# Local attention output in one matmul form for all four batches, under a newly searched instruction order

## The chip, the cores and the metric

The kernel runs on one core of one Trainium2 chip. The metric is device time in microseconds (us) from the first to the last instruction of a run, as the device reports it; the numbers below are medians of runs of the whole kernel. One run of each kernel was also recorded by the hardware profiler, and every row in this document comes from that recording.

## The reference

```python
def _attn_ref(q, k, v):                      # (4, 8, 576, 64)
    factor = 4; Sd = S // factor; scale = 1.0 / np.sqrt(D)
    q_d = q.reshape(B, H, Sd, factor, D).mean(axis=3)      # k_d, v_d alike
    out_d = sm_attn(q_d, k_d, v_d)           # full attention over 144 means
    out_up = np.repeat(out_d, factor, axis=2)
    mask = np.abs(pos[:, None] - pos[None, :]) < factor
    scores = np.where(mask, scale * q @ k.T, -1e9)         # a band of 7 keys
    out_local = softmax(scores) @ v
    return out_up + out_local
x = attention, as 2304 tokens x 512
h = x @ w_in;  g = h * clip(h + 3, 0, 6) / 6;  x = g @ w_out         # d_ff 2048
return max(x @ w1, x @ w2, x @ w3) @ w_out2                          # d_ff 768
```

## The kernel before, in words

**Stages.** There are four batches, b = 0 to 3, and two halves of 288 tokens each. Attention of batch b has a pooled part (`down_scores`, `down_pT`, `down_out`) and a band part (`local_scores`, softmax on DVE and ACT, `local_out`). The two wide layers of the first network follow: for batches 0 and 1 in quarters g = 0 to 3 of the 2048 columns (`moe1_h`, matmuls at L1273, and `moe1_y`, L1311), for batches 2 and 3 by a Strassen-like scheme (L1436 and L1527). The second network, three token groups long, ends the kernel (L1848 and L1957). Large products are made of float16 high and low parts; the attention's are float32.

**The band output.** `local_out(half, e)` multiplies the softmax weights of 12 blocks by 32 keys of v each. One call of it covers two pairs of heads (`cc` = 0, 1, so c = 2e + cc) and the two heads of a pair (`hl` = 0, 1), 48 matmuls of 32 rows by 64 columns in all. A matmul's rows of the array are chosen by c (`tile_position` row 32c) and its columns by hl (column 64 hl). Its result goes to the PSUM tile `pts[cc]`, its moving operand is `pl{half}{hl}`. So in a listing the number of the tile `at` tells the row group and the number of `pl` the column group. In a float32 matmul the trace has two records for one instruction: 96 records are one call. The four batches issue the 48 matmuls in four different orders, chosen by `[b]` at the end of a list of orders; `local_scores` does the same for its matmuls (L964).

**Order.** Every operation is recorded with its number; the text `ORDER` lists the numbers in the order in which they are issued, a star picks the other engine of two that may do an operation (mostly GpSimd in place of VectorE), and `.1` puts in one idle matmul on `warm` (L2091). Each engine then works through its own instructions strictly in that order and waits by semaphores. The costs given to `op(...)` are not read by `schedule`, which only follows `ORDER`.

**The start.** SP issues all DMAs, in order. `load_vw` (L815 to L830) brings v for the band output; for batch 0, half 0 it first clears 32 rows on GpSimd (L815), and SP's own L823 waits for that. Weights arrive as 64-bit numbers: raw tiles `y2` and `y3`, loaded at L1158, are turned to float32 by ACT (L1130), GpSimd (L1132) and DVE (L1135), squared and summed on ACT (L1175) for a scale, and split into high and low float16 parts (ACT L1232, DVE L1234). The softmax of the band ends on DVE with L981 and L984, then L1021 (DVE or GpSimd) and a transpose, L1023. `L1062` adds the band output to the pooled output, and `split` makes x16 of it.

Of the kernel before, what the change touches and what calls it, by code (L numbers as in the profile page):

```python
# [185 lines left out]
0-1 5 7 2 18 22 6 72 23 67 222 38 139 4 213 19-20 9 3 10-11 8 12 15-16 21 13 24 14 17 26 28 25* 35 37 74 36 27  # L186
29 31-33 30 69 86 88 87 89 34 93 68* 92 70* 43 91 44-47 71 98 90 75-76 99 77 94 78 100-101 39 79-80 95 81-82 40
104 103 105 102 48-49 55-56 50 57 51 83 231 73* 96* 214 41 106 216 58 224 215 59 52 97 110 113 60 107 109* 223
53 111 226 54 61 227 62-63 160 115 162 64 161 163 114 112* 108* 116 218 119 118 165 84 167 117 166 85 164 120
65* 66 140 219 172 42 220 217 228 168-169 174 845 225 173 121* 221 175 229 122-123 230 247-248 141 239 178 170  # L190
249 124 250-254 171 235-236 184 176 233 237 177 185 232 179 125-126 234 255-256 127 238 180-181 142-143 187
144-145 391 257 392 128-129 244 183* 241 130 132 131 240 243 245 182 269 186 242 273 135 150-151 146 189 271 275
246 403 276 258-259 393 188 844 397 136* 270 272 147 394 190 148 191 152 260 133 193 192 261 134 277 287 262 395
295 137 194 138* 399 263 195-197 846 288 398 153 264-265 149 266-267 274 154 402 268 859 289-290 282 278 285 198
296-298 400 291 847 155-157 292 158* 303 159 280 283 199 860 405 540 304 293 305 299 281 279 300 311-312 306 313
848 404 201 408 200 314 881 294 849 286 406 301 401 302* 307 284 308 409 315 850 202 862 319-320 316 861 309 317
310* 318* 856 539 851 203 852 209 858 210 857 853 863 321-322 410 323 .1 339 204-206 855 411 407 396 412 207
347-348 208 211 324-325 854 413-414 541 326 329 415-421 212* 542 422-423 543 327 340-342 328 349 343-344 545
334-336 868 424 870 428 865 350 330-332 355 426 351 425 337 864 356-358 345 429 352 867 346* 353 359 338 333 363
427 364 869 926 365-367 360-361 866 433 547 371 871 551 434-436 376 354 927-929 368 873 877 906 550 430 362 546  # L200
548 874 369 441-442 377 372 931 437 875 872 907 438 932 930 933 370* 443 908 431 934 432 935 552 439 449 878 444
373 882 912 883 374 450-451 884-887 375 879 445-446 909 452 556 453 457-458 381-383 459 447 911 914 544 378-380
553 936* 937* 440* 888 876 894 554 889 895 454 915 896 880 558 950 460-461 938 448* 897* 487-488 384 386 939-940
890 489 387 557 385 455 462 941 898 463 891 942 945 944 951 495-496 559 465 953 955 456 892 943 490-491 497-499
388 560 466-467 899 893 464* 900 492 1000 389-390 946 1002 500 901 1001 549 947 952 503-506 954 555 471 511-512
468 1003 1006 493 910* 904* 902 948* 561 916 903 917 1476 472 979 562-564 905 473 513 474 694 565-568 913* 949*
494* 469 569-571 1005 1004 1007 514 980-981 507 475 508 572-573 1008 576 477 956 959-960 515 478 958* 482
982-983 1009 1011* 984-985 990 986 991 483 580-581 484 582 479 688 1477 1487 501 578 509 957 502* 1010* 987 510*
1012 485 480 1475 961* 992 574 516-517 988 1480 588 1478 1481 918 579 583 1479 1482 577 1491 589 1484 689 691
518 481 575 1483 1488 584-585 486 519-522 590 1485-1486 586 919 591 524 690 525 1013 993 526 596 1489 592  # L210
920-921 597 1495 1492 1014 593 1493 695 594 1502 1494 1496 604-606 989 994 598 523 607 922-925 1015 595 1531 692
699 587 1499 529 696 599 1500 1497 600 1490 601 1498 602 962-964 527 697 700 1501 702 608 634 1018 530 1503-1504
635 531 636 965-967 609 968 642-643 1017 1019 1016 610 701 698 528 969 1024 644 532 1027 637 611 533 995 998 703
1020 1551-1552 1021 534-537 1553-1554 1028 538 1029* 1026* 1025 638 970-971 704 972 996* 603* 973 639 1023*
1022* 470 997 1555 1558 1557 1556 1559 612-613 1560 974 645 614 617 640 650 615 646 1534 1030 1033 1032* 1034
999 616 1035 618 1507-1509 1031 1532 1562 1537 1561* 1036 619-620 623 705 693 1539 706-707 1037 647 641 621 708
476 622 1533* 1038 648 1510 709 1511-1513 1575 651 1519 624 652 625-626 1577 1514 710-712 653 1520 1536 1576 713
629-630 714 1521 715 654 627 716-717 1515 718-720 1540 655 1522* 1516* 649* 1563 666 631 1578 1565 1580 1579 721
1517 1564 1566 658-661 1044-1046 722 656 1523 1569 723 1568 662 1518 1047-1048 1524 632 667 731-733 1505 663
1039 1041 1040 739 664 1570 724 1535 734 657 1525 665 668 1567 735 1042 633 725 669 740-742 670 1571 1526 743  # L220
1572 736-737 672 1541 1043 1542 1527 673 1543 747 674 1621 744 1622 1538* 1573* 1544 675 755 748 1623 1545 1053
756 677 1624 1529 1528 1628 1627 1625 749 678 1581 1583* 1626 679 750 757-758 751 1546 759 1530 1601 745
1602-1604 738* 1574* 1629 1547 628 1548 671 746* 728 726 729 752 676 1549 1630 1632* 1672 760 682 1584 680 786
1673 1582 1586* 1585 753 683 794-795 684-685 796 1605 727 1506 681 1631* 1550 754 1606 1587-1588 1611 761 686
975 1589 977 763 787 1612-1614 762* 788-792 730 1607-1608 1590 769-770 764 797 1592 1591 1633 798-800 1635 1634
1636 1593 771-773 1594 1640 801* 1671 978* 765 802 766 1637 1639 1638 793* 810 803 811 1645 812 1647 1683 767
804 1641-1642 976 1685 1644* 775 805 813 1684 1646 806 1677 776 1049 1678 780 777 1674 807-808 1679 1675 687 814
1609 778 1054-1055 1654 1676 815 1680 1610 1056-1057 1656 809 781-783 1062 1686 1690-1691 1058 1655 1059 779
1070 1687 1071 1682 816 1681 1688 1063 1689 1072 1600 1595 817* 1643* 1596-1597 784 818-819 1064 1615-1617 1598
1651 1051 1599 820 1653 1704 1652 1618 1648 821 1695 1650 1619* 1620 1697 1649 822 1060 1692 1065 1696 1073 824  # L230
1657 1066 1658 1061* 1694 1067 1050 823 1052* 768 1659 1693 1068 1078 831 1749 1751 1074 1698 1075 1750 1701 825
1106 826 774 1752 1700 827 1079 832-834 1080 1703 1702 1699 828 1754 1756 1755 1660 1662 1661 1081 1753
1757-1759 837 1107 1663 835 1076 1069* 1077* 1664 1761 1108 1705 838 1109 1086-1088 1773 1082 1708 1729-1730
1083 1735 1084 1706 1763 1760 1762 1707 1764-1765 1768 1766-1767 1114-1117 1776-1777 1774 1110 1778 1775 839
1769 1819-1820 1111 1821 1770 1822 1734 1665 1667 1825 1824 1823 1826 1122 840 1123-1125 1666 1709 1085
1118-1119 1827 1669 1772* 829 1771* 1710 1828 1112 1113* 1829* 1731* 841 1737 1732 1120 1126 1130 1091 1738 1668
1131 1089-1090 1830* 1121* 1127-1128 1129* 836 1711-1714 1779 1092-1093 1715 1782 1094 1096 1781* 1132-1133 1158
1095 1719 1733* 1780 1720 1716 1831 1784 1134 1833 1670 1832 1135 1159 1097 1101-1102 1098 1160-1161 1783 1162
1739 1834 1740-1741 1136 1137* 1736* 1163 1099 1166-1167 1742 1174-1175 1100 1835 1721 1717 1838 1168 1103 1176
1104-1105 1837 1138 1169-1170 1836 1164 1743-1745 1722 785 1746-1748 1785-1786 1718 1723-1724 1727* 1171 1725  # L240
1177 1787 1839 1798 1182-1183 1143-1144 1843 1846 1178 1165* 1840 1868 1179 1139 1844 1140 1184 1841* 1847 1842
1845 1848* 1849 1726 1210 1728 1852 1185 1141 1799 1186 1850 1172 1800-1802 1173 1211-1213 1851* 1142 1187 1854
1853 1180 1855 1803 1856 1804 1809 1218 1145-1146 1148 1805-1806 1181 1214 1857 1807 1147 1808 1810-1811 1188
1788 1790 1789 1149 1791 1153-1155 1792-1793 1795 1812-1813 1215 1814-1815 1794 1796 1226-1228 1219-1221 1216
1816 1817* 1189* 1797 1818 1858 1860 1222 1859 1223 842 1217* 1224-1225 1156 1861-1862 1229 843 1150-1151 1863
# [169 lines left out]
def kernel(  # L415
# [73 lines left out]
    T = {}  # L489
# [1642 lines left out]
```

## Time and profile before

| | |
|---|---|
| median of 3 runs | 789.91 us (789.42 to 791.1) |
| profiled execution | 790.44 us |
| its span on the core | 788.7 us |
| TensorE matmul (PE) busy | 740.1 us, 94% |
| VectorE (DVE) busy | 557.5 us, 71% |
| ScalarE (ACT) busy | 471.1 us, 60% |
| GpSimd (POOL) busy | 304.9 us, 39% |
| mean granted clock of TensorE | 0.97 |

A busy share is a mean over stages with different limits, so each stage has to be read by itself. The profiled execution's own time lies 1.7 us above its span: what stands around the first and the last instruction.

### The profile page before, as it was taken

To read this page: it belongs to the slowest core of one execution; us is meant where nothing else is said; L and a number is where in the kernel's file an instruction comes from. 1 tells how busy PE (TensorE), PEld (TensorE's weight loads), DVE (VectorE), ACT (ScalarE), POOL (GpSimd) and SP (SyncE) were. 2 spreads that over 40 slices of the span, in tenths; PEclk is the share of its full clock that TensorE was granted. 3 is DMA by queue.
4 is the path that set the end of the run, shared out by engine and by line. 5 is a ranking of instruction groups with operands and counts; after the bars stand their busy time and mean duration, and the time that the engine had idled before them with its cause. 6 is when DMAs were issued, how large, how long until landed. Compare 5 with 4: busy or idle time off the path is not lost.

```text
span 788.7 us, 20630 instructions
## 1 busy us (share of the span) xinstructions
PE 740.1 (94%) x8491; PEld 554.3 (70%) x8491; DVE 557.5 (71%) x1139; ACT 471.1 (60%) x1065; POOL 304.9 (39%) x338
## 2 busy tenths in 40 slices
PE   4668899998999999999999999999999999999998
PEld 3455676876777787777777777775555766677667
DVE  1749888788674668888864487368999547852783
ACT  4648899775647535448975588449826441543153
POOL 4525366765433523456342115234654302510050
PEclk9656999999999999999999999999999999999999
DMA  9278856624082000003556333305100010000102
GB/s 259 76 221 229 215 170 168 175 76 82 3 157 74 16 4 2 2 1 101 149 163 197 119 104 110 105 1 173 68 1 2 28 41 14 1 27 1 41 1 94
DMA packets 81248, 68.43 MB, mean 87 GB/s; under 512 B 56962, under 2 KB 68226, under 8 KB 81154
## 3 DMA queue, kind: packets, MB, share of 16 engines
q1 hardware_dynamic: 81154, 67.12, 30.4%
q8 instruction: 66, 1.08, 0.6%
q14 instruction: 28, 0.23, 0.1%
HBM read 56.10 MB, written 11.01 MB: 85 GB/s over the span
## 4 chain that ended last, share of the span: by engine, by line
PE 76%; DVE 12%; ACT 6%; issue 2%; DMA 2%; POOL 1%; SPq 0%; ACTq 0%; DVEq 0%
PE y L1527 12%; PE y L1311 9%; PE h L1273 9%; PE a L1848 8%; PE y L1848 8%; PE at L1957 7%; PE a L1436 6%; PE y L1436 3%; PE h L1848 3%; PE at L1042 2%; PE at L759 2%; PE h L1436 1%; PE a L964 1%; ACT junk L1175 1%; PE at L921 1%
## 5 line engine op out<-in xcount | busy, mean ns | idle before, releaser
L1273 PE MATMUL h<-x,wi 128*128 128x288 f16 x768 | 118.9, 291 | 0.6 <-DVE gf L1288 0.6
L1311 PE MATMUL y<-g,wo 128*128 128x288 f16 x768 | 115.7, 286 | 1.4 <-DVE x L1062 0.7
L1848 PEld LDWEIGHTS <-m2ow 128*128 128x128 f16 x756 | 73.9, 98 | 52.9 <-issue 5.1
L1527 PE MATMUL y<-ga,wo 128*128 128x288 f16 x768 | 96.3, 286 | 0.0
L1527 PEld LDWEIGHTS <-wo 128*128 128x128 f16 x768 | 75.1, 98 | 19.0
L1273 PEld LDWEIGHTS <-wi 128*128 128x128 f16 x768 | 73.7, 99 | 21.0 <-issue 1.8
L1311 PEld LDWEIGHTS <-wo 128*128 128x128 f16 x768 | 72.8, 98 | 21.0 <-issue 3.1
L1848 PEld LDWEIGHTS <-m2w 128*128 128x128 f16 x378 | 36.8, 98 | 22.3 <-DVE hm L1862 0.2
L1293 POOL TENSOR_TENSOR g<-gf,g 128x288 f16<-128x288 f32 x34 | 29.6, 872 | 50.4 <-ACT g L1291 37.3
L1132 POOL TENSOR_SCALAR z<-z 128x384 int32<-128x384 uint32 (+1 forms) x36 | 22.8, 632 | 62.3 <-DMA z<-in_moe_w_dram 37.9
L1848 PE MATMUL y<-yb,m2ow 128*128 128x384 f16 x234 | 43.6, 326 | 2.2 <-DVE hm L1862 1.7
L1848 PE MATMUL a<-yb,m2ow 128*128 128x384 f16 x234 | 43.4, 326 | 1.4 <-DVE hm L1862 0.7
L1436 PEld LDWEIGHTS <-S 128*128 128x128 f16 x384 | 37.4, 98 | 9.6 <-issue 0.2
L1135 DVE SCALAR_TENSOR_TENSOR zo<-zo,z 128x384 int32<-128x384 int32 (+1 forms) x36 | 21.1, 587 | 21.0 <-ACT zo L1130 16.0
L1957 PE MATMUL at<-m2fw,hm 128*128 128x256 f16 x288 | 35.0, 272 | 0.6 <-DVE y L1976 0.6
L1957 PEld LDWEIGHTS <-hm 128*128 128x128 f16 x324 | 31.7, 98 | 5.5 <-issue 1.0
L1291 ACT CAST g<-gf 128x288 f16<-128x288 f32 x64 | 27.3, 430 | 12.8 <-DVE gf L1288 10.0
L1436 PEld LDWEIGHTS <-wi 128*128 128x128 f16 x288 | 28.2, 98 | 7.1
L1346 POOL TENSOR_TENSOR m2fw<-hm 128x384 f32<-128x384 f32 x7 | 7.9, 1140 | 57.1 <-DVE hm L1862 48.7
L1284 ACT ACTIVATE r<-h,sc 128x288 f32<-128x288 f32 x32 | 18.8, 592 | 18.4 <-PE h L1273 18.4
L871 ACT ACTIVATE pd<-a,dsm 72x144 f32<-72x144 f32 x60 | 22.1, 376 | 11.5 <-DVE dsm L865 9.2
L759 PE MATMUL at<-ident,stg 128*128 128x128 f32 x128 | 22.2, 314 | 7.1 <-DVE stg L656 2.3
(331 smaller groups left out, 1824.5 us busy)
## 6 DMA issues: line engine op xcount, KB each, us to landing
z<-in_moe_w_dram SPq DMA_DIRECT2D x24, 384.0 KB, 3.3
y<-in_moe_w_in_dram SPq DMA_DIRECT2D x8, 1024.0 KB, 5.8
y<-in_moe_w_out_dram SPq DMA_DIRECT2D x8, 1024.0 KB, 5.3
vw<-in_v_dram SPq DMA_DIRECT2D x62, 96.0 KB, 4.1
out_dram<-y SPq DMA_DIRECT2D x18, 256.0 KB, 2.2
stg<-in_k_dram SPq DMA_DIRECT2D x6, 512.0 KB, 6.0
stg<-in_q_dram SPq DMA_DIRECT2D x6, 512.0 KB, 7.1
stg<-in_v_dram SPq DMA_DIRECT2D x6, 512.0 KB, 4.6
```

The lines of the kernel that those rows point to most:

```text
L759: nc.tensor.transpose(out=po[:, i, :, f], in_=T[n(f"{nm}{kc}{c // 2}")][:, f, 2 * (c % 2):2 * (c % 2) + 2, :], identity=ident[0:nr, 0:nr])
L871: op("ACT", c_act(SD, 2) - 0.01, prio, lambda i=i, j=j, x=x: nc.scalar.activation(out=T[pds[j]][:, i], in_=view(j)[:, i], func=AF.Exp, bia ...
L1132: op("POOL", c_f32(n), prio, lambda: nc.gpsimd.tensor_scalar(out=words()[0], in0=words()[0].bitcast(U32), scalar1=0.8735 * 2.0 ** -29, sca ...
L1135: op("DVE", c_dve(n), prio, lambda: nc.vector.scalar_tensor_tensor(out=dst().bitcast(I32), in0=dst().bitcast(I32), scalar=3, in1=words()[0 ...
L1273: nc.tensor.matmul(out=hp(), lhsT=T[wt][:, a, kk, i * P:i * P + P], rhs=T[x16][:, e, kk, :], start=(kk == 0 and (a, e) == (0, 0)), stop=(k ...
L1291: op("ACT", c_act(CH, 0, False), prio + LEAD, lambda: nc.scalar.copy(out=T[g16][:, 0], in_=T[gf]), r=[gf], w=[(g16, 0)], new=[buf(g16, "ac ...
L1293: op("DVE", c_dve(CH), prio + LEAD, lambda e: e.tensor_tensor(out=T[g16][:, 1], in0=T[gf], in1=T[g16][:, 0], op=ALU.subtract), r=[gf, (g16 ...
L1311: nc.tensor.matmul(out=T[acc][:, 0:CH], lhsT=T[wt][:, a, i, d * P:d * P + P], rhs=T[gs[i]][:, e], start=(i == 0 and (a, e) == (0, 0)), sto ...
L1436: nc.tensor.matmul(out=ps_(x)(), lhsT=lhs(a, kt), rhs=T[xn][:, e, kt, :], start=(first and kt == 0 and (a, e) == (0, 0)), stop=(kt == 1 an ...
L1527: nc.tensor.matmul(out=T[acc][:, 0:CH], lhsT=T[wt][:, a, 2 * fb + i, d * P:d * P + P], rhs=hl[:, e * S + half * CH:e * S + half * CH + CH] ...
L1848: nc.tensor.matmul(out=b(to), lhsT=w_op(nm, o)[:, a, kt, fp * P:fp * P + P], rhs=T[f"yb{p}{y}"][:, e, kt, :], start=(first and kt == 0 and ...
L1957: nc.tensor.matmul(out=ps_(x)(), lhsT=h_op(p, fp, o)[:, a, i * P:i * P + P], rhs=T["m2wo"][:, j, e, fp, :], start=(first and fp == 0 and ( ...
```

## The change: one form, and another order

Three things are edited. `local_out` now issues its 48 matmuls in the one order that batch 1 had; `local_scores` in the one that batch 0 had. Two costs given to the planner are lowered, which `schedule` doesn't read. `ORDER` is replaced as a whole (141 lines); of its numbers one line stands here before and after, since numbers tell a reader little. The new one has two entries `.1` where the old one had one.

```diff
-0-1 5 7 2 18 22 6 72 23 67 222 38 139 4 213 19-20 9 3 10-11 8 12 15-16 21 13 24 14 17 26 28 25* 35 37 74 36 27
...
+3874 3854 3878 3855-3858 3884-3887 3879 3888 3880-3883
...
             for kc in range(2):
-                op("PE", 0.7, prio, lambda kc=kc: pe(kc), duty=0.36, ni=32,
+                op("PE", 0.6, prio, lambda kc=kc: pe(kc), duty=0.36, ni=32,
...
                     for o, nq in spans_:
-                        for hl, c in (
-                                [(hl, c) for hl in range(2) for c in range(4)],
-                                [(hl, c) for c in range(4) for hl in range(2)],
-                                [(c % 2 ^ x, c) for x in range(2) for c in range(4)],
-                                [(hl, c) for c in (0, 2, 1, 3) for hl in range(2)])[b]:
-                            nc.tensor.matmul(
...
+                        for hl in range(2):
+                            for c in range(4):
+                                nc.tensor.matmul(
...
             def pe(j):
                 ii, two = range(4 * j, 4 * j + 4), range(2)
-                for i, hl, cc in (
-                        [(i, hl, cc) for i in ii for cc in two for hl in two],
-                        [(i, cc ^ x, cc) for i in ii for x in two for cc in two],
-                        [(i, hl, cc) for hl in two for i in ii for cc in two],
-                        [(i, hl, cc) for cc in two for i in ii for hl in two])[b]:
+                for i, hl, cc in [(i, cc ^ x, cc) for i in ii for x in two for cc in two]:
...
             for j in range(3):
-                op("PE", 0.6, prio, lambda j=j: pe(j), duty=0.11, ni=64,
+                op("PE", 0.48, prio, lambda j=j: pe(j), duty=0.11, ni=64,
```

In the changed kernel lines after the 955th stand 3 to 6 lower: L964 is L961, L1042 is L1036, L1135 is L1129, L981 is L979, L984 is L982, L1158 is L1152. Lines between 189 and 955 stand 1 higher.

**TensorE, the band output.** Batch 2, half 1, before: the column group (`pl`) stays while the row group (`at`) alternates.

```order
L1042 MATMUL at_3885<-pl_3741,vw1_3652 64x24
L1042 MATMUL at_3886<-pl_3741,vw1_3652 64x24
L1042 MATMUL at_3885<-pl_3741,vw1_3652 64x24
L1042 MATMUL at_3886<-pl_3741,vw1_3652 64x24
L1042 MATMUL at_3885<-pl_3741,vw1_3652 64x24
```

Batch 3, half 1, before: the row group stays while the column group alternates.

```order
L1042 MATMUL at_4962<-pl_4881,vw1_4484 64x24
L1042 MATMUL at_4962<-pl_4886,vw1_4484 64x24
L1042 MATMUL at_4962<-pl_4881,vw1_4484 64x24
L1042 MATMUL at_4962<-pl_4886,vw1_4484 64x24
L1042 MATMUL at_4962<-pl_4881,vw1_4484 64x24
```

The same call in the changed kernel:

```order
L1036 MATMUL at_4959<-pl_4875,vw1_4373 64x24
L1036 MATMUL at_4960<-pl_4877,vw1_4373 64x24
L1036 MATMUL at_4959<-pl_4877,vw1_4373 64x24
L1036 MATMUL at_4960<-pl_4875,vw1_4373 64x24
L1036 MATMUL at_4959<-pl_4875,vw1_4373 64x24
```

Now the row group changes from each matmul to the next, and the column group with it in every other step.

**VectorE, the end of the first band softmax** (batch 0, half 0), before: from the second sum to the end of the softmax (`mx`, `sm`) nothing of the weights stands between; the four conversions at L1135 come behind both transposes.

```order
L1016 TENSOR_REDUCE mx_277<-sm_276 128x12
L877 RECIPROCAL dsm_362<-dsm_362 72x4
L1016 TENSOR_REDUCE mx_277<-sm_275 128x12
L981 TENSOR_SCALAR mx_277<-mx_277 128x24
L984 RECIPROCAL mx_277<-mx_277 128x24
L1021 TENSOR_TENSOR sm_275<-sm_275,mx_277 128x384
```

And now:

```order
L1014 TENSOR_REDUCE mx_242<-sm_240 128x12
L1014 TENSOR_REDUCE mx_242<-sm_241 128x12
L631 TENSOR_SCALAR sc_88<-tiny_90 128x1
L1129 SCALAR_TENSOR_TENSOR wi3_420<-wi3_420,y2_154 128x512 x2
L1129 SCALAR_TENSOR_TENSOR wi3_420<-wi3_420,y3_150 128x512 x2
L979 TENSOR_SCALAR mx_242<-mx_242 128x24
L909 TENSOR_TENSOR pT_432<-at_488,which_86 32x144
L982 RECIPROCAL mx_242<-mx_242 128x24
L1019 TENSOR_TENSOR sm_240<-sm_240,mx_242 128x384
```

The four weight conversions moved ahead of L981 and L984 (now L979 and L982). On GpSimd the clearing of `vw0` (L815) still stands right behind that half's L1021.

**SP, the queue of loads**, before: the raw tiles `y` of w_in, v for the band (`vw`), and the raw tiles of w_out behind them.

```order
L1158 DMA y_154<-in_moe_w_in_dram 128x2x512
L664 DMA wo_156<-in_q_dram 64x8x64
L830 DMA vw_158<-in_v_dram 32x12x64 x8
L1158 DMA y_173<-in_moe_w_in_dram 128x2x512
L823 DMA vw_535<-in_v_dram 29x64
L830 DMA vw_535<-in_v_dram 32x11x64
L830 DMA vw_535<-in_v_dram 32x12x64 x7
L703 DMA stg<-in_k_dram 128x16x64
L1158 DMA y_579<-in_moe_w_out_dram 128x2x512
L1158 DMA y_600<-in_moe_w_out_dram 128x2x512
```

And now:

```order
L1152 DMA y_150<-in_moe_w_in_dram 128x2x512
L665 DMA wo_152<-in_q_dram 64x8x64
L1152 DMA y_154<-in_moe_w_in_dram 128x2x512
L831 DMA vw_561<-in_v_dram 32x12x64 x8
L704 DMA stg<-in_k_dram 128x16x64
L824 DMA vw_572<-in_v_dram 29x64
L831 DMA vw_572<-in_v_dram 32x11x64
L831 DMA vw_572<-in_v_dram 32x12x64 x7
L1152 DMA y_583<-in_moe_w_out_dram 128x2x512
L1152 DMA y_698<-in_moe_w_out_dram 128x2x512
```

The second half of w_in moved ahead of the first eight loads of v, and the load of batch 1's k moved from behind the second group of v loads to ahead of it.

## Rows read from the trace of the kernel before

**Rows 1.** The page: granted clock in 40 slices; the chain that ended last

```profile
PEclk9656999999999999999999999999999999999999
...
PE 76%; DVE 12%; ACT 6%; issue 2%; DMA 2%; POOL 1%; SPq 0%; ACTq 0%; DVEq 0%
```

**Rows 2.** Windows: stretch, length, busy us of PE, PEld, DVE, ACT, POOL; granted clock

```profile
0.00:22.00 22.00, 10.18 (x92) 7.99 (x95) 4.74 (x10) 9.85 (x19) 11.24 (x33) 1.00 1.02 253
25.70:73.40 47.70, 30.96 (x574) 22.96 (x575) 34.85 (x101) 28.82 (x76) 18.18 (x25) 0.50 0.55 157
240.00:300.00 60.00, 60.00 (x1325) 48.17 (x1322) 38.56 (x99) 33.80 (x96) 22.63 (x28) 1.00 0.08 18
500.00:540.00 40.00, 40.00 (x311) 30.25 (x309) 24.96 (x42) 23.94 (x34) 15.14 (x10) 1.00 0.31 106
540.00:610.00 70.00, 66.85 (x410) 39.78 (x408) 67.23 (x109) 44.58 (x75) 37.13 (x25) 1.00 0.09 32
```

**Rows 3.** Timeline of PE: band output, one call in batches 0, 1, 2, 2, 3

```profile
85.24 1.59 PE L1042 MATMUL y<-pl,vw 32*64 32x24 f32 x96
154.41 1.59 PE L1042 MATMUL at<-pl,vw 32*64 32x24 f32 x96
224.73 2.29 PE L1042 MATMUL at<-pl,vw 32*64 32x24 f32 x96
238.61 2.16 PE L1042 MATMUL at<-pl,vw 32*64 32x24 f32 x96
279.84 1.98 PE L1042 MATMUL at<-pl,vw 32*64 32x24 f32 x96
```

**Rows 4.** Timeline of PE: band scores, one block of 64 in batches 1 and 3

```profile
106.82 0.76 PE L964 MATMUL a<-kT,qT 64*32 64x32 f32 x64
252.82 0.76 PE L964 MATMUL a<-kT,qT 64*32 64x32 f32 x64
```

**Rows 5.** Timeline of SP, 19 to 46 us: the queue of loads

```profile
37.20 0.28 SPq L823 DMA_DIRECT2D vw<-in_v_dram  x1
37.52 5.24 SPq L830 DMA_DIRECT2D vw<-in_v_dram  x8
42.87 0.63 SPq L703 DMA_DIRECT2D stg<-in_k_dram  x1
43.61 1.80 SPq L1158 DMA_DIRECT2D y<-in_moe_w_out_dram  x2
```

**Rows 6.** SP's own waits, 0 to 110 us: total, times, longest

```profile
SPq L823 <- POOL vw L815: 17.1, 1, 17.1
```

**Rows 7.** Timeline of DVE, 28 to 66 us

```profile
33.98 0.30 DVE L984 RECIPROCAL mx<-mx 128x24 f32<-128x24 f32 x1
37.73 1.84 DVE L1135 SCALAR_TENSOR_TENSOR wi<-wi,y 128x512 int32<-128x512 int32 x3
55.72 0.94 DVE L1062 SCALAR_TENSOR_TENSOR x<-h,sc,od 128x288 f32<-128x288 f32 x2
```

**Rows 8.** Timeline of POOL, 34 to 38 us

```profile
35.41 0.83 POOL L1021 TENSOR_TENSOR sm<-sm,mx 128x384 f32<-128x384 f32 x1
...
37.03 0.14 POOL L815 MEMSET vw<- 32x64 f32 x1
```

**Rows 9.** The chain that ended last, 43 to 72 us: start, length, what

```profile
43.61 8.22 DMA y<-in_moe_w_out_dram
```

**Rows 10.** DMA issues by line: count, KB each, median us to landing

```profile
y<-in_moe_w_out_dram SPq DMA_DIRECT2D x8, 1024.0 KB, 5.3
```

**Rows 11.** Timeline of PE, 61 to 76 us: the first dense stretch

```profile
67.06 2.38 PE L921 MATMUL at<-pT,vd 128*64 128x72 f32 x32
69.38 4.36 PE L1273 MATMUL h<-x,wi 128*128 128x288 f16 x18
```

**Rows 12.** Waits of PE, 90 to 300 us: total, times, longest

```profile
PE at L1042 <- ACT pT L897: 1.1, 1, 1.1
```

**Rows 13.** Waits of PE, 500 to 789 us: total, times, longest

```profile
PE y L1848 <- DVE hm L1862: 1.7, 1, 1.7
```

More of the change, by code (lines that the diff above doesn't have):

```diff
@@ new lines @@
+2233 2123 2158 2139 2142 2128 2451 2140 2124 2127 2227 2229 2228 2154-2155 2452 2160 2159 2164 2143-2144 2129
+2161 2224 2230 2157 2145 2165 2146 2130 2234 2236 2235 2237 2148 2150 2232 2149 2240 2162 2453 2460-2461
+2454-2455 2231 2456 2147* 2151-2152 2167 2163 2241 1474 2243 2153 2168 2242 2166 2171 2238 2172 2169 2244
+2173-2175 2170 2462 2457 2463-2464 2239 2465 2248 2247 2250 2527 2249 2245 2176 2251 2458 2246 2252 2459
+2466-2467 2254 2468 2470-2476 2255 2479 2531* 2477 2480-2482 2256-2259 2261 2483-2486 2253 2260 2268 2262 2264
@@ L345 @@
+3811-3812 3761 3832 3836 3788-3790 3808 3837-3838 3841 3809 3839 3762 3810 3791 3783 3792 3794 3793 3842 3813
+3843 3815 3814 3795 3816-3817 3819-3820 3796 3818 3824-3826 3844 3797 3821 3849 3822 3827 3850 3560 3823 3851
+3828 3859-3861 3863-3865 3840 3862 3867-3869 3852 3870 3866 3845-3847 3875-3876 3871-3872 3848 3873 3877 3853
+3874 3854 3878 3855-3858 3884-3887 3879 3888 3880-3883
 """
@@ L958, in pe @@
                     for o, nq in spans_:
-                        for hl, c in (
-                                [(hl, c) for hl in range(2) for c in range(4)],
-                                [(hl, c) for c in range(4) for hl in range(2)],
-                                [(c % 2 ^ x, c) for x in range(2) for c in range(4)],
-                                [(hl, c) for c in (0, 2, 1, 3) for hl in range(2)])[b]:
-                            nc.tensor.matmul(
-                                out=T[names[hl]][32 * c:32 * c + nq, i * 32:i * 32 + 32],
-                                lhsT=T[n("qT")][64 * hl:64 * hl + 64, c, o:o + nq],
-                                rhs=T[n("kT")][64 * hl:64 * hl + 64, c, t0:t0 + 32],
-                                start=not on_pe,
-                                stop=not on_pe or i == 10,
-                                tile_position=(64 * hl, 32 * c))
+                        for hl in range(2):
+                            for c in range(4):
+                                nc.tensor.matmul(
+                                    out=T[names[hl]][32 * c:32 * c + nq, i * 32:i * 32 + 32],
+                                    lhsT=T[n("qT")][64 * hl:64 * hl + 64, c, o:o + nq],
+                                    rhs=T[n("kT")][64 * hl:64 * hl + 64, c, t0:t0 + 32],
+                                    start=not on_pe,
+                                    stop=not on_pe or i == 10,
+                                    tile_position=(64 * hl, 32 * c))
             for j in range(6):
```

309 lines of the change are left out of this document (151 added, 158 removed).

## The prediction, before the changed kernel had run

> **What bounds the kernel now.** I read the page first, then the busy times by stretch, the timelines of the engines over the first 76 us, and last the waits of TensorE and of SP. The page's chain is 76% TensorE (PE) and its clock row is full but for slices in the first tenth [rows 1]. The stretches say it apart [rows 2]. From 240 to 300 us and from 500 to 540 us PE is busy without a gap: there every us of matmul time taken out is a us of the kernel. From 540 to 610 us PE and VectorE (DVE) are both nearly full. [...] The start is a chain of DMAs and small operations, in which SP stands still for 17.1 us because GpSimd has not yet cleared 32 rows of `vw0` [rows 6].
>
> **The band output in one form.** The trace holds the price of all four forms, since each batch has its own. One call of 48 matmuls took 1.59 us in batch 0 and 1.59 us in batch 1, 2.29 and 2.16 us in two calls of batch 2, and 1.98 us in batch 3 [rows 3], all at full clock. The new form is that of batch 1. So batches 0 and 1 gain nothing. Batch 2 gains 2.22 - 1.59 = 0.63 us in each of four calls, 2.5 us; batch 3 gains 1.98 - 1.59 = 0.39 us in each of four, 1.6 us. Together 4.1 us. The calls shown of batches 2 and 3 run from 224 us on, and from 240 us PE has no gap [rows 2] in which a gain could be lost. The first calls of batch 0 run in the half-clock stretch, where the trace has no price of the new form; they wait for other engines there, and I take nothing for them.
>
> [...]
>
> **The scores in one form.** A block of 64 records took 0.76 us in batch 1's form and 0.76 us in batch 3's [rows 4]; the single form costs and saves nothing. The two lowered planner costs are not read; the second `warm` matmul stands behind batch 0's second band-output call, in the start where PE mostly waits, and without that wait it would cost some 0.5 us (two records at the 0.24 us of the 18 of [rows 11]).
>
> **The new order at the start.** Three pieces count. First, on DVE four conversions (L1135) come ahead of L981 and L984. Three of them took 1.84 us [rows 7], so four cost 2.45 us, and two maxima that moved along make it some 3: L984 ends near 37.3 us in place of 34.3. Behind it queue GpSimd's L1021 (0.83 us), the clearing, and SP. Before, GpSimd only came to L1021 at 35.41 us and cleared at 37.03, with a conversion in between [rows 8]; the new order has no conversion there, so the clearing comes at about 37.3 + 0.83 + 0.1 = 38.2 us, 1.2 later. Second, SP then issues the `vw0` loads (0.28 + 5.24 us) and now w_out directly, since the load of k has moved ahead: 0.63 + 0.1 us are saved [rows 5]. So w_out is issued at about 44.0 us in place of 43.6, 0.4 later. Third, that k load, half the size of one w_out piece, no longer stands ahead of w_out in the transfers. The first w_out piece took 8.22 us to land [rows 9]; the median of its kind is 5.3 us [rows 10]. I take the middle, 6.7 us: 1.5 gained. Net, w_out lands 1.1 us earlier; the bounds are 2.5 earlier (5.3 us) and 0.8 later (8.22 us, and L984 another 0.4 later).
>
> What is behind that landing is the same work before and after: conversion of w_out on DVE, which holds up L1062 (at 55.72 us before [rows 7]), the second half of the band output, x16, and the first dense stretch of PE at 69.38 us [rows 11]. I keep its length. DVE has other work between, one split more here and a conversion fewer there, in pieces of about a us (the L1062 pair: 0.94 [rows 7]); so 1 us to either side.
>
> **The new order later.** The same matmuls are issued, in groups that change as often between small and full array forms. Single waits of PE that hang on the order are 1.1 us before 300 us [rows 12] and 1.7 us after 500 us [rows 13]. Each may go, or come elsewhere; I take zero, with 2.8 us to either side. Somewhat more of the optional work stands on DVE now, mostly in stretches where PE is full and DVE has room, such as 500 to 540 us, with 25 of 40 us busy [rows 2].
>
> **The sum.** 4.1 + 1.1 = 5.2 us off the profiled execution's 790.44 us gives 785.2. That execution lay 0.5 us above the median of 789.91, so the median becomes 784.7 us. The bounds: 4.1 + 2.5 + 1 + 2.8 = 10.4 us gained, 779.5; and 4.1 - 0.8 - 1 - 2.8 = 0.5 us lost, 790.4.
>
> **The rivals.**
> [...]
> *The gain stops at the DVE stretch.* DVE is busy 67.2 of 70 us from 540 to 610 [rows 2]; if its work there were ready regardless of PE, PE's 5 us would turn into waiting there, leaving about 789.5 us. Against it: DVE has 15 us of idle time in the 40 us ahead, so it waits for what PE and the buffers that PE frees hand on.
> *The forms were not the cause.* Form and batch go together in the trace. If batches 2 and 3 were slow for another reason, only 1.1 us is left: 788.8 us. Against it: batch 1 and batch 2 use the same tiles at the same clock.
> *Slower: the clearing of `vw0` is held up.* The four L1135 now ahead of L984 need GpSimd's and ACT's halves of the conversion. If one of these is late, DVE waits in order, and with it L984, GpSimd's clearing, SP, w_out and all behind, us for us. From a clearing at 45.0 us on (38.2 + 6.8) the kernel is slower by over 0.2%; at 46 us it would take 792.5 us. Against it: w_in's second half is loaded earlier now, and SP had waited 17 us, so that the raw data is long there.
>
> **How the numbers follow.** The forecast, a few us gained from the forms and about one from the start, gets 0.57; the earlier clock 0.14, the DVE stretch 0.08, the forms 0.07, the held clearing 0.08, and 0.06 is left for a second fall of the clock or a new wait, half of it slower. A difference under 0.2%, 1.6 us, can't be told from none here. Faster: most of the forecast (0.53), the clock (0.14), half of the third rival and a little of the others: 0.76. Same: 0.13. Slower: 0.11. The range is that of the bounds, 779.5 to 790.0; it takes in the clock and the two rivals near no change, and leaves out the held clearing and what is below 779.5.
>
> **What would show it.** Right: every band-output call at full clock takes about 1.6 us; score blocks stay at 0.76; L815 runs near 38 us and w_out is issued near 44 and lands near 51; the dense stretch begins near 68 us and the clock rises soon after; PE is full from 240 us on, everything there 5 us earlier. Wrong: calls near 2 us in batches 2 and 3; a clearing beyond 40 us; a clock of 0.50 after 75 us; new waits of PE of more than 2 us in one place.

## The result, and the profile after

The changed kernel takes 780.29 us (median of 4 runs, 780.03 to 782.58) where the kernel before took 789.66 on the same chip: a ratio of 0.9884, 95% interval 0.9864 to 0.9903. That is 9.4 us gained where 5.2 were predicted. The direction and the range held; the terms of the sum did not, and that the range held owes something to luck, as shown below. The profiled execution took 780.03 us, 10.4 less than the one before.

The page of the changed kernel: busy tenths of TensorE, granted clock, the chain that ended last, and one of the DMA queues (packets, MB, share).

```profile
PE   5658979999999999999999999999999999999998
...
PEclk9658999999999999999999999999999999999999
...
q8 instruction: 66, 1.08, 0.6%
...
PE 76%; DVE 4%; ACT 2%; issue 2%; POOL 1%; DVEq 0%; POOLq 0%; ACTq 0%
```

Against [rows 1], VectorE's share of the chain fell from 12% to 4%, and the granted clock reads 8 in the fourth slice, where it read 6. The line q8 is needed in the experiments. The same stretches as in [rows 2], in the same columns:

```profile
0.00:22.00 22.00, 12.82 (x180) 9.99 (x180) 6.78 (x12) 11.27 (x22) 12.14 (x33) 1.00 0.99 283
25.70:73.40 47.70, 33.17 (x613) 24.80 (x613) 37.63 (x94) 34.52 (x87) 20.96 (x27) 0.58 0.54 165
240.00:300.00 60.00, 59.81 (x1304) 47.80 (x1302) 42.93 (x103) 32.07 (x91) 17.09 (x21) 1.00 0.14 31
540.00:610.00 70.00, 68.30 (x435) 42.36 (x434) 66.99 (x114) 43.01 (x77) 42.22 (x25) 1.00 0.07 23
```

TensorE does 2.6 us more work in the first 22 us. The same matmuls can be found in both traces, so one can work out by how much the changed kernel is ahead when it starts the same one: some 5 us at 30 us, 7.6 at 98, then only 3.0 at 110 and 1.9 at 150, 8.0 at 293, and 10.7 at the end. Since the orders differ, these hold to about half a us, less well where matmuls changed places. So the start gained far more than I had put down, and three quarters of it was given back between 98 and 150 us, before the forms added theirs.

The band output, to be held against [rows 3] (batches 1, 2, 2, 3), and a block of band scores against [rows 4]; timeline of TensorE (in this trace the scores stand at L962 and the softmax's first step at L1004, two lines above L964 and L1006):

```profile
153.65 1.59 PE L1036 MATMUL at<-pl,vw 32*64 32x24 f32 x96
219.37 1.59 PE L1036 MATMUL at<-pl,vw 32*64 32x24 f32 x96
236.60 1.59 PE L1036 MATMUL at<-pl,vw 32*64 32x24 f32 x96
279.70 1.59 PE L1036 MATMUL at<-pl,vw 32*64 32x24 f32 x96
...
128.12 0.76 PE L962 MATMUL a<-kT,qT 64*32 64x32 f32 x64
```

Every whole call at a granted clock of 1.00 takes 1.59 us, and the scores 0.76, as predicted.

The start, from the timelines of SP, GpSimd, ScalarE and TensorE (to be held against [rows 5, 8, 9, 11]):

```profile
36.52 0.17 POOL L816 MEMSET vw<- 32x64 f32 x1
...
36.72 0.30 SPq L824 DMA_DIRECT2D vw<-in_v_dram  x1
37.07 4.78 SPq L831 DMA_DIRECT2D vw<-in_v_dram  x8
41.95 0.93 SPq L1152 DMA_DIRECT2D y<-in_moe_w_out_dram  x2
...
47.41 1.21 ACT L1124 ACTIVATE wo<-y 128x512 f32<-128x512 f32 x2 [6.29 <-DMA y<-in_moe_w_out_dram]
...
60.71 2.39 PE L922 MATMUL at<-pT,vd 128*64 128x72 f32 x32
63.03 3.40 PE L1267 MATMUL h<-x,wi 128*128 128x288 f16 x15
```

The clearing comes at 36.52 us, not at 38.2; w_out is issued at 41.95, and its first piece has landed by 47.41, 5.5 us later, where it took 8.22 before: 4.4 us earlier in all. The dense stretch begins at 63.03 us in place of 69.38.

And the place where it went back: timelines of TensorE, VectorE and ScalarE near 107 us.

```profile
101.08 1.51 PE L962 MATMUL a<-kT,qT 64*32 64x32 f32 x154
107.03 0.80 PE L962 MATMUL a<-kT,qT 64*32 64x32 f32 x54 [4.44 <-issue]
...
108.46 2.52 PE L1305 MATMUL y<-g,wo 128*128 128x288 f16 x12
...
119.80 0.53 PE L1305 MATMUL y<-g,wo 128*128 128x288 f16 x3 [1.33 <-ACT y L1316]
...
107.89 1.02 DVE L1004 TENSOR_TENSOR sm<-a,cap 128x384 f32<-128x384 f32 x2 [6.34 <-PE a L962]
...
116.82 0.38 ACT L770 ACTIVATE qT<-at 128x256 f32<-128x256 f32 x1 [3.16 <-DVE qkd L803]
```

TensorE stands still for 4.44 us in the middle of one run of 208 score records (104 matmuls, two records each), put down to "issue": nothing that the profile shows was waited for. VectorE idles 6.34 us for those scores, ScalarE 3.16 us for VectorE, and TensorE once more, 1.33 us for ScalarE. Right behind the first wait, matmuls of 288 columns take 0.2 us and more each, where 0.12 is usual; the granted clock from 105 to 110 us was 0.69. In the kernel before, the same 208 records stood as 64 and 144 with dense work between, and the wait was 1.06 us:

```profile
110.80 0.61 PE L964 MATMUL a<-kT,qT 64*32 64x32 f32 x47 [1.06 <-issue]
```

### The profile page after: what moved, and what is told of

The parts are those of the page before. It is cut to its first block, busy times and chain, and to the rows that moved or that the text cites. A ratio compares the mean times of both kernels' runs of the same rounds, so it can differ in the third digit from the quotient of the medians.

```text
span 778.2 us, 20629 instructions
## 1 busy us (share of the span) xinstructions
PE 737.7 (95%) x8493; PEld 552.5 (71%) x8493; DVE 564.5 (73%) x1151; ACT 467.8 (60%) x1067; POOL 294.2 (38%) x325
## 3 DMA queue, kind: packets, MB, share of 16 engines
q8 instruction: 66, 1.08, 0.6%
## 4 chain that ended last, share of the span: by engine, by line
PE 76%; DVE 4%; ACT 2%; issue 2%; POOL 1%; DVEq 0%; POOLq 0%; ACTq 0%
PE y L1521 12%; PE a L1842 10%; PE y L1842 9%; PE y L1305 8%; PE h L1267 8%; PE at L1951 7%; PE a L1430 6%; PE h L1842 3%; PE y L1430 3%; PE at L1036 2%; PE h L1430 2%; PE a L962 1%; PE at L922 1%; PE at L760 1%; PE a L1951 1%
## 5 line engine op out<-in xcount | busy, mean ns | idle before, releaser
L1267 PE MATMUL h<-x,wi 128*128 128x288 f16 x768 | 116.0, 290 | 2.7 <-DVE gf L1282 2.4
L1305 PE MATMUL y<-g,wo 128*128 128x288 f16 x768 | 114.1, 288 | 1.6 <-ACT y L1316 1.3
L1267 PEld LDWEIGHTS <-wi 128*128 128x128 f16 x768 | 73.5, 99 | 23.1 <-issue 4.0
L1287 POOL TENSOR_TENSOR g<-gf,g 128x288 f16<-128x288 f32 x38 | 33.0, 870 | 59.4 <-ACT g L1285 56.7
L1129 DVE SCALAR_TENSOR_TENSOR zo<-zo,z 128x384 int32<-128x384 int32 (+1 forms) x36 | 22.9, 639 | 22.1 <-ACT zo L1124 10.8
L1285 ACT CAST g<-gf 128x288 f16<-128x288 f32 x64 | 27.0, 427 | 15.6 <-DVE gf L1282 14.7
L1126 POOL TENSOR_SCALAR y<-y 128x1024 int32<-128x1024 uint32 (+1 forms) x20 | 22.3, 1114 | 18.0 <-DMA y<-in_moe_w_out_dram 15.4
L1430 PE MATMUL a<-x,S 128*128 128x288 f16 x192 | 28.6, 286 | 0.0
L1430 PE MATMUL y<-x,S 128*128 128x288 f16 x192 | 28.3, 286 | 0.0
```

The source lines that it names most:

```text
L1126: op("POOL", c_f32(n), prio, lambda: nc.gpsimd.tensor_scalar(out=words()[0], in0=words()[0].bitcast(U32), scalar1=0.8735 * 2.0 ** -29, sca ...
L1129: op("DVE", c_dve(n), prio, lambda: nc.vector.scalar_tensor_tensor(out=dst().bitcast(I32), in0=dst().bitcast(I32), scalar=3, in1=words()[0 ...
L1267: nc.tensor.matmul(out=hp(), lhsT=T[wt][:, a, kk, i * P:i * P + P], rhs=T[x16][:, e, kk, :], start=(kk == 0 and (a, e) == (0, 0)), stop=(k ...
L1285: op("ACT", c_act(CH, 0, False), prio + LEAD, lambda: nc.scalar.copy(out=T[g16][:, 0], in_=T[gf]), r=[gf], w=[(g16, 0)], new=[buf(g16, "ac ...
L1287: op("DVE", c_dve(CH), prio + LEAD, lambda e: e.tensor_tensor(out=T[g16][:, 1], in0=T[gf], in1=T[g16][:, 0], op=ALU.subtract), r=[gf, (g16 ...
L1305: nc.tensor.matmul(out=T[acc][:, 0:CH], lhsT=T[wt][:, a, i, d * P:d * P + P], rhs=T[gs[i]][:, e], start=(i == 0 and (a, e) == (0, 0)), sto ...
```

## The experiments

Times are medians on the chip of that run. The kernel before had 789.28 us beside the first four, 789.19 beside the next four, 791.11 beside the three after them and 790.85 beside the last, so kernels that were timed beside different ones of these are compared by their ratios to it. Numbers in ORDER are plan steps.

**1 and 2. The forms alone, the order alone.** The first kernel is the one before with this edit; the second is the changed kernel with the same edit turned round.

```diff
-                for i, hl, cc in (
-                        [(i, hl, cc) for i in ii for cc in two for hl in two],
-                        [(i, cc ^ x, cc) for i in ii for x in two for cc in two],
-                        [(i, hl, cc) for hl in two for i in ii for cc in two],
-                        [(i, hl, cc) for cc in two for i in ii for hl in two])[b]:
+                for i, hl, cc in [(i, cc ^ x, cc) for i in ii for x in two for cc in two]:
```

> The kernel before with one edit: the band output's matmuls are issued in the one form of the change in every batch; order and scores stay as before. My term for the form: batches 2 and 3 lose 0.63 and 0.39 us in each of four calls, so 4.1 us less than the kernel before, 785.6 us in place of 789.7, with calls of 1.6 us. [...] Rival, form and batch only coincide: calls stay at 2.2 and 2.0 us, 789.7.

> The changed kernel with one edit: the band output goes back to its four forms, one for each batch; the new order and the one form of the scores stay. If the two parts of the change add up, this is 4.1 us slower than the changed kernel, 784.4 us, and the order alone is then worth 789.7 - 784.4 = 5.3 us, where I had put 1.1. Rival: the order was searched for the new form, and with the old ones new waits appear: 786 or more.

Measured: the form alone 787.05 us, ratio 0.9965 (0.9949 to 0.9981), 2.8 us gained; the order alone 783.85 us, ratio 0.9927 (0.9903 to 0.9952), 5.8 us gained. Together 8.6, and the whole change 9.2 by its ratio: within their intervals the parts add up. The one form of the scores is in the second kernel, with the order; it was not run by itself, and all there is for it are its blocks of 0.76 us. The band output of batch 2 in TensorE's timeline, with the form alone:

```profile
221.63 1.90 PE L1038 MATMUL at<-pl,vw 32*64 32x24 f32 x96
235.12 1.77 PE L1038 MATMUL at<-pl,vw 32*64 32x24 f32 x96
```

and with the order alone, in batches 2 and 3:

```profile
240.02 1.98 PE L1040 MATMUL at<-pl,vw 32*64 32x24 f32 x96
276.43 1.98 PE L1040 MATMUL at<-pl,vw 32*64 32x24 f32 x96
```

So batch 2's old form costs 1.98 us, as batch 3's does. The 2.29 and 2.16 of [rows 3] held 0.31 and 0.18 us that stay with the old order under either form (1.90 and 1.77 over 1.59); what they are was not found.

**3 and 4. The run of scores cut, and made.** One kernel cuts the changed kernel's run of 208 records; the other makes such a run in the kernel before.

```diff
-445 878 452 376 373 377 556 912 931 934 873 374 431 453 552 375 544 935 446-447 882-887 936* 910*
+445 878 452 376 882-883 373 377 556 912 931 934 873 374 431 453 552 375 544 935 446-447 884-887 936* 910*
```

```diff
-444 373 882 912 883 374 450-451 884-887 375
+444 373 882 912 883-887 374 450-451 375
```

> The changed kernel with one edit in the order: the first two of the six score blocks of batch 1's first half are issued four steps of dense work earlier (ahead of the steps 373, 377 and 374), so that the run of 208 score records is cut into 64 and 144. Theory A: the 4.4 us wait of TensorE at 107 us comes from the run itself, which eats its instructions faster than they are brought in; in two pieces the wait falls to some 1.1 us, as in the kernel before, and with the short fall of the clock behind it the time falls by 3 to 5 us, to 775.3 to 777.3. Theory B: the wait belongs to that moment (a transfer or another engine), whatever stands there; it stays at 3 us or more and the time within 1 us of 780.3.

> The kernel before with one edit in the order: the three steps of dense work (374, 450, 451) that stand between the second and the third score block of batch 1's first half are issued behind the sixth, so that 208 score records follow one another as in the changed kernel. Theory A (the length of the run makes the wait): TensorE's wait in the run grows from 1.1 to between 3 and 4.5 us, the time by 2 to 4 us, to 791.7 to 793.7. Theory B (the moment makes it): the wait stays near 1.1 us and the time within 0.8 us of 789.7.

Measured: cut, 782.07 us, ratio 0.9905 (0.9876 to 0.9934), not faster than the change; made, 791.88 us, ratio 1.0031 (1.0014 to 1.0048), 2.4 us slower. TensorE in the first:

```profile
102.28 0.97 PE L962 MATMUL a<-kT,qT 64*32 64x32 f32 x90
106.00 0.80 PE L962 MATMUL a<-kT,qT 64*32 64x32 f32 x54 [2.75 <-issue]
```

and in the second:

```profile
105.67 1.64 PE L964 MATMUL a<-kT,qT 64*32 64x32 f32 x170
109.42 0.54 PE L964 MATMUL a<-kT,qT 64*32 64x32 f32 x38 [2.10 <-issue]
```

Both waits moved the way of theory A, and neither as far as it said. What gives the cause away is the x54: cut or not, the wait ends 54 records before the end of the run, at the same instruction. Counted in the traces of the six kernels run by then, the waits for issue inside runs of small matmuls stand whole multiples of 256 TensorE instructions apart (matmuls, weight loads and semaphore instructions counted). The page has the size: 66 packets of q8 carry 1.08 MB, 16.4 KB each, and 8,493 matmuls with as many weight loads make 257 instructions to a packet. How many packets' worth of instructions are held ahead, no run here shows.

So the theory became: the instructions come in blocks of 256, whose borders are called seams here; a block is asked for when TensorE reaches a seam, and if the block in hand is run through sooner than the next one arrives, TensorE stands still at the next seam. A block of score records alone takes some 1.3 us (154 records took 1.51). In the DMA records of the trace, the packet belonging to the 4.44 us wait begins at 104.54 us and takes 1.16; TensorE goes on at 107.03, 1.3 us behind its end. In the kernel with the run made, the packet takes 1.33 us from 106.81, and TensorE goes on at 109.42, again 1.3 us behind its end. In the kernel before and in experiments 3, 5, 6, 10 and 12 that distance is 1.3 to 1.5 us too, so the restart hangs on the packet. When a block is asked for is less sure: behind the restart at 107.03 us the next packet began 1.0 us later, but in dense work of the same trace one began at 87.67, 1.1 us ahead of the seam, which TensorE reached at 88.76.

**5 and 6. The seams moved by half a block, and by a whole one.** Both put filler ahead of the program, 32 and 64 tiny matmuls.

```diff
+        for _ in range(32):
+            nc.tensor.matmul(out=T["tail"][0:32, CH:CH + 16], lhsT=warm[0:32, 0:32], rhs=warm[0:32, 0:16],
+                             start=True, stop=True)
```

> The changed kernel with 32 tiny matmuls (64 records, so 128 of TensorE's instructions with their weight loads) put ahead of everything, where TensorE waits 5.6 us for its first input anyway; the order is untouched. Counted in the traces of six kernels, every wait in the middle of a run of small matmuls that is put down to issue stands a whole multiple of 256 TensorE instructions from the others (the 449th, 1217th, 2753rd, 3521st, 4545th, 6081st, 8641st). Theory A: instructions come in blocks of 256, and a wait arises where a whole block runs faster than the next is brought; half a block of filler moves the seams so that none lies behind a block of score records alone: the 4.4 us wait goes, the waits for issue from 90 to 250 us fall from 6.2 us to about 1, and the time falls by 4 to 5 us against the changed kernel, to some 776 us. Theory B (the wait belongs to the moment or to the run as such): it stays, and the time is the changed kernel's 780.3 or a little more.

> The control of the run with 128 filler instructions: 64 tiny matmuls (256 instructions, one whole block) ahead of everything, so the seams lie where they lay in the changed kernel. Theory A: the wait in the score run is back at 3.5 to 5 us and the time within 1 us of the changed kernel's 780.3. If instead the filler itself does something (the array's clock, the start), this kernel gains as much as the one with half a block.

Measured: half a block 778.31 us, ratio 0.9883 (0.9849 to 0.9916); a whole one 782.09 us, ratio 0.9912 (0.9894 to 0.9930). TensorE with half a block:

```profile
99.45 1.96 PE L962 MATMUL a<-kT,qT 64*32 64x32 f32 x208
101.33 0.54 PE L1267 MATMUL h<-x,wi 128*128 128x288 f16 x3
101.71 1.02 PE L1305 MATMUL y<-g,wo 128*128 128x288 f16 x7
105.39 1.17 PE L1305 MATMUL y<-g,wo 128*128 128x288 f16 x5 [2.66 <-issue]
```

and with a whole one:

```profile
108.00 1.51 PE L962 MATMUL a<-kT,qT 64*32 64x32 f32 x154
113.57 0.67 PE L962 MATMUL a<-kT,qT 64*32 64x32 f32 x54 [4.06 <-issue]
```

The place of the wait is settled. With the seams moved by half a block, 208 score records run through without a stop, and TensorE now waits ten matmuls behind them, between two of the same dense run, for nothing but the seam. With a whole block the wait is back, after 154 records as in the changed kernel. The gain is not settled: the medians differ by 3.8 us, but the intervals overlap, and half a block's ratio is that of the change, to which one of its six times, 786.94 us against 777.43 to 780.33 for the others, adds much. I had expected 4 to 5 us; the wait shrank only to 2.66, since this block too, mostly scores, runs through in some 2.5 us (5.2 us from seam to seam with the wait).

**7. The scores spread.**

```diff
-376 373 377 556 912 931 934 873 374 431 453 552 375 544 935 446-447 882-887 936* 910* 894 888-889 895 440 457
-378-379 381-382 458-460 432 890 380
+376 882 373 377 883 374 556 912 931 934 873 431 453 552 375 544 935 446-447 936* 910* 440 884 457
+378-379 885 381-382 458-460 886-887 894 888-889 895 432 890 380
```

> The changed kernel with one edit in the order: the six score blocks of batch 1's first half are issued with dense work between all of them (33 matmuls of the steps 373 to 460 in the run, in place of none). Theory A: the block of 256 instructions that held score records alone now holds some 33 dense matmuls (4 us) and 95 small records (1.1 us), about 5 us in all, and the wait of 4.4 us falls below 1 us; the time falls by 3 to 5 us, to some 776 us. Theory B: the wait stays at 3 us or more.

Measured: 780.95 us, ratio 0.9900 (0.9870 to 0.9931). The 4.44 us wait is gone, and the time is the change's. Matched matmul for matmul, TensorE is some 4 us ahead of the changed kernel at 110 us, 0.9 at 122 and 0.5 at 128. TensorE, VectorE and ScalarE show where it went:

```profile
115.66 0.32 PE L891 MATMUL at<-ident,pd 72*128 72x72 f32 x2 [1.05 <-ACT qT L770]
118.12 0.88 PE L1305 MATMUL y<-g,wo 128*128 128x288 f16 x3 [1.34 <-ACT y L1316]
...
108.09 1.02 DVE L1004 TENSOR_TENSOR sm<-a,cap 128x384 f32<-128x384 f32 x2 [5.22 <-PE a L962]
...
115.13 0.38 ACT L770 ACTIVATE qT<-at 128x256 f32<-128x256 f32 x1 [3.16 <-DVE qkd L803]
```

VectorE still gets its last scores at 108 us, and in its queue behind their softmax stands the reduction of a q transpose (L803) that TensorE had long finished; ScalarE's copy of the same transpose (L770) waits for that reduction, and TensorE waits for ScalarE. The new order had put both steps there (554 880 879 557); in the kernel before, the copy (879) had its place ahead of that softmax, and the reduction (880) had not.

**8. The k load put back.**

```diff
-140 139 845 42 230
+140 139 42 845 230
```

> The changed kernel with one edit in the order: the load of batch 1's k goes back behind the loads of vw0, just ahead of w_out, as in the kernel before. If the missing k load is what made the first w_out piece land in 5.4 us where it took 8.22, then here it is issued 0.6 us later, lands after some 8 us again, 3.4 us later in all, and the dense stretch begins 2 to 3.4 us later; the time grows by up to that much, less where TensorE would only have waited for its instructions at 107 us: 780.5 to 783.7 us. Rival: the landing is set by something else (the load of w_in's second half, which the change also moved): landing stays near 5.4 us and the time within 1 us of 780.3.

Measured: 783.26 us, ratio 0.9929 (0.9910 to 0.9948), 3.6 us above the change by the ratios. SP, ScalarE and TensorE:

```profile
43.10 0.63 SPq L704 DMA_DIRECT2D stg<-in_k_dram  x1
43.83 2.28 SPq L1152 DMA_DIRECT2D y<-in_moe_w_out_dram  x2
...
50.78 1.21 ACT L1124 ACTIVATE wo<-y 128x512 f32<-128x512 f32 x2 [8.36 <-DMA y<-in_moe_w_out_dram]
...
66.45 3.78 PE L1267 MATMUL h<-x,wi 128*128 128x288 f16 x15
```

w_out is issued 1.9 us later and lands 7.0 us after that in place of 5.5; both landing and dense stretch are 3.4 us late, the end of the profiled execution 3.1. (1.3 us of it stood already at 38 us, ahead of the moved load.) So of the 3.4 us the load itself has 2.1, 0.6 in the queue and 1.5 in the landing; by the whole time it is worth 2 to 3.5 us.

**9 to 12. The q steps put back ahead, and w_in.** Three kernels carry the same edit, on the spread scores (9), on half a block of filler (10) and on the changed kernel itself (12):

```diff
-878 452 376
+878 452 376 879-880
...
-554 880 879 557-558
+554 557-558
```

> The kernel with the score blocks spread among dense work, with one more edit: the copy and the reduction of the last q transpose (steps 879 on ScalarE and 880 on VectorE) are issued right behind that transpose, ahead of the score softmax, as in the kernel before. Theory: spreading took the 4.4 us wait away, but what TensorE gained (4.4 us at 110 us) was down to 0.5 us at 128 us, because VectorE still idles 5.2 us for the last score block with the q reduction queued behind it, ScalarE's q copy waits for that reduction (3.2 us), and TensorE waits for the q copy (1.1 us) and for ScalarE's next y (1.3 us). With the q steps ahead these two waits go: 2 to 3 us less than with the spreading alone, 778 to 779 us. Rival: the softmax chain itself sets the pace to 120 us; waits only change their names and the time stays within 1 us of 781.

> The kernel with half a block of filler, with the same edit: the copy and the reduction of the last q transpose right behind that transpose. In that kernel ScalarE waited 4.3 us for VectorE's q reduction and TensorE 1.3 us for ScalarE's y at 117 us. Theory: both go, 1.3 to 2 us less than with the filler alone, 776.3 to 777 us, and so faster than both kernels of the change. Rival: what was gained is waited for at the next place; within 0.8 us of 778.3.

> The changed kernel with the q edit alone: the copy and the reduction of the last q transpose (879 on ScalarE, 880 on VectorE) right behind that transpose; score run and seams stay as they were. Theory A (two faults one behind the other): the 4.4 us wait in the score run stays and holds the softmax as long as before; only the waits behind it go, 1.3 us at ScalarE's y and what hangs on it, so 1 to 2 us less than the changed kernel, a ratio to the kernel before of 0.986 to 0.987, some 4 us short of what the q edit and either cure of the wait reached together (0.982 and 0.980). Theory B (the place of the q steps was the whole of it): the ratio reaches 0.982 with the 4.4 us wait still there.

Measured: on the spread scores 776.41 us, ratio 0.9824 (0.9804 to 0.9845); on the filler **775.53 us, ratio 0.9803 (0.9779 to 0.9827)**; alone 779.21 us, ratio 0.9861 (0.9838 to 0.9883). By the ratios the edit gains 6.0 us on the spread scores, where 2 to 3 were expected. The second is 15.6 us faster than the kernel before and, by the ratios, 6.4 faster than the change; its interval lies clear of the change's. TensorE, VectorE and ScalarE in it:

```profile
105.67 0.77 PE L1305 MATMUL y<-g,wo 128*128 128x288 f16 x5 [2.73 <-issue]
...
101.67 1.02 DVE L1004 TENSOR_TENSOR sm<-a,cap 128x384 f32<-128x384 f32 x2 [1.28 <-PE a L962]
...
98.44 0.38 ACT L770 ACTIVATE qT<-at 128x256 f32<-128x256 f32 x1
```

and in the kernel with the q edit alone:

```profile
107.64 0.80 PE L962 MATMUL a<-kT,qT 64*32 64x32 f32 x54 [4.93 <-issue]
```

Alone, the q edit leaves the wait in the scores (4.93 us) and gains 1.8 us by the ratios, within the 1 to 2 expected; its interval overlaps the change's. On the filler it gains more than the 1.3 to 2 expected. The scores are not the reason: with the filler alone VectorE already had them at 101.47 us. Two things are. Behind the 2.73 us TensorE has no other wait up to 122 us, where the filler alone had 1.34 us for ScalarE at 116.99. And the clock does not fall. With the filler alone, then with the q edit on it (columns as in [rows 2]):

```profile
105.00:109.00 4.00, 3.61 (x17) 2.25 (x16) 1.91 (x4) 0.88 (x3) 0.83 (x1) 0.58 0.47 109
```

```profile
105.00:109.00 4.00, 3.33 (x30) 2.45 (x30) 2.26 (x6) 2.53 (x5) 2.24 (x3) 1.00 0.36 81
```

Behind nearly the same wait the same five matmuls take 1.17 us at the low clock and 0.77 without its fall. With the filler alone the clock fell once more, to 0.57 from 119 to 123 us. Worked out from the two timelines, the two falls cost some 3 us, more than the waits that went. With the q edit alone the granted clock was 0.61 from 105 to 110 us and 0.71 from 110 to 115, where the changed kernel had 0.69 and 0.97, so there the clock took back a part of what the edit gave.

So these are two faults in a row, of which curing either alone shows little: the first cure's gain was waited for at the second, and a part of either was lost to the low clock behind a wait that was left. That the clock follows from the waits is read from one trace of each kernel, and was not tested alone.

The last kernel asked what else of the start counted:

```diff
-222 38 213 4 7
+222 38 139 213 4 7
...
-140 139 845 42
+140 845 42
```

> The changed kernel with one edit in the order: the load of the second half of w_in goes back behind the eight loads of vw1, as in the kernel before; the k load stays ahead. Theory: this load is the other half of what the new start gained. It is issued some 9 us later, its raw data lands near 29 us, the four conversions on VectorE that now stand ahead of L982 wait for GpSimd's and ScalarE's parts of it, and the clearing of vw0, at 36.5 us in the changed kernel, comes at 38.5 to 40 us; w_out and the dense stretch move by the same 2 to 3.5 us, and the time with them: 782.3 to 783.8 us. Rival: the conversion has slack; the clearing stays within 0.7 us and the time within 1 us of 780.3.

Measured: 782.15 us, ratio 0.9883 (0.9864 to 0.9903), the change's own. GpSimd and TensorE:

```profile
36.52 0.14 POOL L816 MEMSET vw<- 32x64 f32 x1
...
63.40 3.78 PE L1267 MATMUL h<-x,wi 128*128 128x288 f16 x15
```

The clearing has not moved, though SP issued that load at 18.52 us and not at 9.57. The theory falls: w_in's second half has at least some 9 us of slack. The slower rival, a held-up clearing, falls with it.

## Why the prediction was right in direction and off in size

**The band output.** Right in mechanism; 4.1 us was put down. The form's own price is 1.98 - 1.59 = 0.39 us a whole call in both batches (experiment 2), not 0.63 in batch 2: I read as form what stayed with the order there. Two calls of batch 2 run in two pieces, where the forms differ by 0.25 (0.91 to 0.66) and 0.32 (1.45 to 1.13). That makes 2 x 0.39 + 2 x 0.57 + 4 x 0.39 = 3.5 us; the runs give 2.8 (form alone) and 3.4 (0.9927 - 0.9884, in 789 us). "Forms were not the cause" falls with them.

**What else sets the forms apart.** At the same order batch 2's form, whose row group changes with every matmul, costs 1.98 us, no less than batch 3's, whose row group stays (experiment 2): a changing row group alone did not make a call short. By the lists in the kernel, the two forms of 1.59 us go round all four pairs of row and column group, and the two of 1.98 us go back and forth between two of them. No run tells this apart from other differences between the forms.

**The start: 1.1 us was put down, 7.6 stood there at 98 us.** This is the mis-sized term. Up to the landing of w_out 4.4 us were gained, in two steps. The clearing was to come 1.2 us later and came 0.5 earlier. The four conversions do stand ahead of L982, and at 2.48 us they cost what I had put down, but VectorE began the first softmax (L1004, L1006 before) at 25.28 us where it had begun at 28.33, since the scores ahead of it came 3 us earlier; I had counted what was put into the queue and not that the queue starts sooner. And the landing took 2.8 us less, where I had put down 1.5 for the absence of the k load. Experiment 8 gives 1.5 back (7.0 us against 5.5), so the k load was sized right; what took the other 1.3 off was not found. Then there is the length behind the landing, which I had kept with 1 us to either side: of the 7.6 us, 3.2 came there, and no run takes them apart. What was gained before 20 us was not tested by itself.

**The later order: zero was put down, 5.7 us went back between 98 and 150 us.** The list of what would show me wrong had "new waits of PE of more than 2 us in one place": 4.44 us came. That waits hang on the count of instructions no row said. But the wait itself stood at the head of the list from which [rows 12] is taken, longer in total than the one I named (waits of PE, 90 to 300 us):

```profile
PE a L964 <- issue: 1.9, 2, 1.1
```

I passed over it, and put down nothing for a wait that the trace already had. From 150 to 293 us the lead then grew by 6.1: 3.5 by the forms, and the rest not taken apart further; the 1.1 us wait of [rows 12] is among what went. So the range held in part by luck: the start gained 6.5 us more than was put down, and the later order gave most of it back in between. (The range's upper end stands as 790.0, where its sum gives 790.4; nothing hangs on that.) From 540 us on came 2.7 more, where [rows 13] had 1.7 us and the new order has 0.9. The rival of a gain lost at the VectorE stretch has nothing for it: the lead was 8.0 us at 293 us and 10.1 at 605.

**The clock.** That the clock would rise ahead of the first dense stretch, to which I had given 0.14, did not come: the granted clock of 0.50 ended at 66 us in place of 73.5, 2.9 us into the dense stretch, where before it was 4.1 us. The 1.2 us less at 0.50 are worth some 0.6 us, an estimate from 0.50 against the 1.00 that follows. What brings the clock up, no run here shows. It did fall again, to 0.69 from 105 to 110 us, behind the 4.44 us wait; TensorE was busy 2.97 us of those 5.

## What to carry to other kernels

Count instructions where matmuls are tiny: a block of 256 holds 128 of their records with as many weight loads and ran through in 1.3 us here, and from seam to seam, wait included, it took 3 to 6 us, so work of some us has to stand between such runs. A wait marked "issue" that ends at the same instruction in two kernels was a seam here; half a block of filler moved it, a whole one did not. And where removing a wait gains nothing, compare both traces matmul by matmul to see where the lead is handed back: the second fault stands there. Read the granted clock behind each wait as well: with the filler, the low clock cost some 3 us, an estimate, more than the waits that the q edit took away.

## What the runs showed of the hardware that was not expected

- From seam to seam, wait included, 256 instructions took some 5.7 us in the changed kernel (128 score records and 4.44 us), and some 3.4 in the kernel with the run made (the same and 2.10). In the first, transfers of up to 437 GB/s ran from 101.9 to 104.6 us, and the packet of instructions began at 104.54, as they ended. In the kernel before, the packet began 0.7 us after TensorE had reached the seam ahead of the wait, with 56 GB/s moving meanwhile; in the changed kernel 3.3 us after it, with 331, and in experiments 3, 5, 10 and 12 between 2.6 and 3.7 us after it, with 273 to 392. That other transfers held it up fits all of these, and was not tested alone.
- Some executions of the same kernels record a granted clock of 1.00 from the first microsecond. The busy times by stretch of the kernel with spread scores and the q edit, and of the changed kernel (columns as in [rows 2]):

```profile
25.00:62.00 37.00, 24.97 (x529) 19.11 (x510) 26.25 (x80) 25.04 (x71) 17.41 (x24) 1.00 0.56 161
```

```profile
25.00:62.00 37.00, 24.68 (x502) 18.52 (x502) 26.90 (x78) 24.79 (x70) 16.00 (x23) 0.50 0.56 159
```

  At 1.00 and at 0.50 the band output's 94 records take 2.76 us in either. So that figure is not the clock at which those matmuls ran (in the first trace no clock record stands ahead of 67.1 us); the durations of a known shape are the better witness.
